# Window attention, forward and backward: one 64x64-mode stretch a step instead of two, weights turned straight from DRAM, and weight-gradient tail over five PSUM banks

## The chip, the cores and the metric

The kernel runs on one core of one Trainium2 chip. The metric is the device time of one execution in microseconds (us), the median over several runs. A run's state is "fast" where it agrees with the other runs of its kernel, and "unknown" for a single run; no run of this study fell in the slow state, and the mean granted TensorE clock of a run lies between 0.98 and 1.00 in all of them (it was lower for short stretches, see run 1). TensorE is called PE below, its weight load PEld, VectorE DVE, ScalarE ACT, GpSimd POOL, and SyncE SP. SP computes nothing here; it issues DMAs. PS in the code is PSUM, the memory that TensorE's products are written to: eight banks of 512 columns. To evict a bank is to copy it out by ACT or DVE.

## The reference, cut to what matters

```python
def _fwd_reference(x, wqkv, wo):                 # x (1,256,256,384), 8x8 windows
    xw = ...                                     # (1024 windows, 64 tokens, 384)
    qkv = xw @ wqkv
    q, k, v = ...
    p = _softmax(jnp.einsum('bqc,bkc->bqk', q, k) * C ** (-0.5), axis=-1)
    o = jnp.einsum('bqk,bkc->bqc', p, v) @ wo
    return ...                                   # back to (1,256,256,384)

def reference(x, wqkv, wo, grad_out):            # all bf16
    _out, _vjp = jax.vjp(_fwd_reference, x, wqkv, wo)
    return (_out, *_vjp(grad_out))               # out, dx, dwqkv, dwo
```

The kernel folds the weights once (A = scale Wq Wk^T, B = Wv Wo, and both transposed). It then works on 128 "quads" of four tiles; a tile is two windows, 128 tokens by 384 channels.

## The kernel before

Each turn of the loop ("step n") works on three quads at once. Quad n (T) gets its outputs, its transposed-attention products and its input gradient, quad n+1 (S) its scores and softmax, and quad n+2 (A) its two projections. SP issues everything that comes in: eight loads of 96 KB a step (four X, four DO), then four DMA transposes, called "turns" here: XT and DOT from the inputs, and two YH turns that turn the projections' results back. POOL issues the stores: four OS stores (out) and eight DXS stores (dx).

```python
def load(n):
    for t in range(4):
        SP.dma_start(out=X[:, (n % NX) * 4 + t, :], in_=img(x, n, t))
        SP.dma_start(out=DO[:, (n % ND) * 4 + t, :], in_=img(grad_out, n, t))

def turn_in(n):            # ... cut: xs, ds are the four tiles of the quad
    SP.dma_start_transpose(out=XT[:, n % NXT, :, :], in_=xs)
    SP.dma_start_transpose(out=DOT[:, n % NDT, :, :], in_=ds)

def turn_yh(n, a):
    SP.dma_start_transpose(out=YH[:, n % NTOK, a, :, :], in_=YHT[...])

def proj(n, a, banks, engs):   # three PSUM banks, each evicted to YHT by its engine
    ...
def attn(n, t, bvw, bdx):      # 64x64 mode: eight 64x384 products of one tile
    ...
def step(n):
    T, S, A = n, n + 1, n + 2
    ...                        # cut: load(n + 4), turn_in(n + 3)
    scores(S); chain1(S); md(T)
    wgrad(g, k0)               # 12 products into bank 7
    chain2(S); chain3(S)
    outs(T, 0, 0, ACT); outs(T, 2, 2, DVE); outs_st(T)
    proj(A, 0, (4, 5, 0), (ACT, DVE, ACT)); turn_yh(A, 0)
    wgrad(g, k0 + 1)
    attn(T, 0, 2, 4); attn(T, 1, 0, 5)          # first 64x64 stretch
    dxs(T, 0, 4, ACT); dxs_st(T, 0)
    proj(A, 1, (2, 3, 1), (DVE, ACT, DVE)); turn_yh(A, 1)
    turn_p(S)                                   # second 64x64 stretch ...
    attn(T, 2, 2, 4); attn(T, 3, 0, 5)
    dxs(T, 2, 4, ACT); dxs_st(T, 2)
```

(The conditions for the first and last steps and the evictions of VW are cut. `scores` and `chain1` to `chain3` make the softmax and its gradient; `md` makes the factor MD, from which `outs` makes the output and `dxs` a part of dx; `attn` makes the rest of dx and VW, from which `wgrad` sums the weight gradients. In 64x64 mode, `64*64` in the trace, TensorE's array works as four parts of 64 rows by 64 columns.)

## Time and profile before

The time is 2079.63 us, median of three runs (2079.23 to 2081.49). These lines of the profile's page give the span, the busy time of each engine with its share, then the busy tenths of the 16 DMA engines in 40 slices, the shares of the engines in the chain of work that ended last, and for the OS stores their number, size and median time in us from issue to landing.

```profile
span 2072.7 us, 65934 instructions
PE 2029.9 (98%) x26970; PEld 1149.4 (55%) x26970; DVE 1358.6 (66%) x2452; ACT 985.1 (48%) x1555; POOL 1012.9 (49%) x1798
DMA  8999999999999999999999999999999999999991
PE 96%; DMA 2%; SPq 2%; DVE 0%; ACT 0%; issue 0%; DVEq 0%
out_dram<-OS POOLq DMA_DIRECT2D x512, 96.0 KB, 2.9
```

PE: 98% busy and 96% of the chain. The waits of PE for the turned input are few, as this line of the waits view says (us in total, times, longest), and all five fall before 100 us:

```profile
PE PS L73 <- DMA XT<-X: 10.2, 5, 3.5
```

The DMA row stands at 9 in nearly every slice. The timeline of SP's queue in one steady step (start, length of the issue):

```profile
1001.81 5.21 SPq L101 DMA_TRANSPOSE YH<-YHT  x2
1007.08 0.59 SPq L91 DMA_DIRECT2D X<-in_x_dram  x1
1007.75 0.55 SPq L92 DMA_DIRECT2D DO<-in_grad_out_dram  x1
...
1011.68 0.55 SPq L92 DMA_DIRECT2D DO<-in_grad_out_dram  x1
1012.28 2.47 SPq L96 DMA_TRANSPOSE XT<-X  x1
1014.80 2.58 SPq L98 DMA_TRANSPOSE DOT<-DO  x1
```

A load takes SP about 0.6 us, a turn 2 to 3 us, and each issue starts within some 0.1 us of the end of the one before. (The time that SP waits for another engine lies before such a record and not in it: in run 4, where SP does wait, the second YH turn is recorded from 0.025 us after the end of the eviction that it needs, in all of 90 steps looked at.)

Here are the stages of one step, the mean over the middle steps, from the start of one stage's first product to the start of the next. They are worked out from the start times of the products in the trace.

| stage | before, us | after, us |
|---|---|---|
| scores | 0.878 | 1.180 |
| md | 0.797 | 0.797 |
| wgrad, first | 1.960 | 1.960 |
| outs | 1.950 | 1.950 |
| wgrad, second | 2.043 | 2.460 (1.950 when nothing waits) |
| proj0 | 1.943 | 2.043 |
| 64x64 stretches | 0.777 and 1.214 | 1.987 |
| dxs | 0.987 and 1.079 | 1.976 |
| proj1 | 2.036 | 2.036 |
| whole step, mean | 15.66 | 16.38 |

The mode switches hide in the last product of a stage: 128x384 products follow each other at 0.162 us, but the last one before a 64x64 stretch takes 0.256.

### The profile page before, as it was taken

What the parts mean: (1) busy time and instruction counts of PE and PEld (TensorE: products, weight loads), DVE (VectorE), ACT (ScalarE), POOL (GpSimd) and SP (SyncE); (2) the same over time, 40 slices, a digit from 0 to 9 for tenths busy, and PEclk for the clock granted to TensorE, in tenths of its full rate; (3) what the DMA queues carried; (4) which work ended last, traced back from release to release, by engine and by line L of the source; (5) the groups of instructions that cost most, each with busy time, mean ns of one, the idle gap of its engine ahead of it and who ended that gap; (6) DMA issues with size and microseconds to landing.
All of it is one profiled execution on the core that took longest, in us unless ns stands there. A gap on an engine that the chain in (4) does not pass through costs nothing.

```text
span 2072.7 us, 65934 instructions
## 1 busy us (share of the span) xinstructions
PE 2029.9 (98%) x26970; PEld 1149.4 (55%) x26970; DVE 1358.6 (66%) x2452; ACT 985.1 (48%) x1555; POOL 1012.9 (49%) x1798
## 2 busy tenths in 40 slices
PE   5899999999999999999999999999999999999997
PEld 2455555555555555555555555555555555555554
DVE  3566666666666666666666666666666666666664
ACT  2444444444445444444444444544444444444452
POOL 1454555555555455455555555545545555555552
PEclk9999999999999999999999999999999999999999
DMA  8999999999999999999999999999999999999991
GB/s 177 203 202 202 208 201 197 209 205 198 205 207 200 204 206 200 202 209 198 206 200 205 203 204 203 202 203 205 200 201 208 202 201 204 206 204 200 206 177 56
DMA packets 1030734, 410.90 MB, mean 198 GB/s; under 512 B 865056, under 2 KB 1013280, under 8 KB 1030432
## 3 DMA queue, kind: packets, MB, share of 16 engines
q1 hardware_dynamic: 956304, 305.37, 84.1%
q0 software_dynamic: 73728, 101.02, 18.2%
q8 instruction: 212, 3.47, 0.7%
q14 instruction: 90, 0.74, 0.1%
q10 hardware_dynamic: 400, 0.29, 0.0%
HBM read 101.84 MB, written 101.84 MB: 98 GB/s over the span
## 4 chain that ended last, share of the span: by engine, by line
PE 96%; DMA 2%; SPq 2%; DVE 0%; ACT 0%; issue 0%; DVEq 0%
PE PS L73 94%; PE PS L150 2%; DMA XT<-X 1%; SPq L92 0%; SPq L91 0%; SPq L231 0%; DMA VW<-in_wo_dram 0%; DVE ACC L219 0%; SPq L233 0%; ACT DXS L77 0%; ACT YHT L77 0%; SPq L98 0%; DVE YHT L79 0%; SPq L96 0%; PE PS L310 0%
## 5 line engine op out<-in xcount | busy, mean ns | idle before, releaser
L207 POOL DMA_DIRECT2D out_dram<-DXS x1024 | 572.8, 566 | 583.7 <-ACT DXS L77 561.4
L73 PE MATMUL PS<-VW,X 128*128 128x384 bf16 x3072 | 542.7, 326 | 4.5 <-DVE ACC L219 4.5
L73 PEld LDWEIGHTS <-X 64*64 64x64 bf16 (+1 forms) x9216 | 380.3, 104 | 218.8 <-issue 6.9
L79 DVE CAST YHT<-PS 128x512 bf16<-128x512 f32 x384 | 264.3, 688 | 240.4 <-PE PS L73 238.4
L73 PEld LDWEIGHTS <-MD 128*128 128x128 bf16 x3072 | 279.3, 98 | 232.4 <-issue 61.5
L77 ACT CAST VW<-PS 128x768 bf16<-128x768 f32 x256 | 204.3, 798 | 367.6 <-PE PS L73 367.6
L77 ACT CAST YHT<-PS 128x512 bf16<-128x512 f32 x384 | 224.7, 585 | 277.6 <-PE PS L73 253.7
L219 DVE TENSOR_TENSOR ACC<-PS,ACC 128x384 f32<-128x384 f32 x252 | 140.5, 558 | 257.3 <-PE PS L73 257.3
L73 PE MATMUL PS<-AT_sb,MD 128*128 128x384 bf16 x1536 | 294.1, 328 | 0.0
L141 POOL TENSOR_TENSOR UM<-PB,ST 128x256 f32<-128x256 bf16 x128 | 77.8, 608 | 424.1 <-PE PS L73 367.8
L73 PE MATMUL PS<-XT,A_sb 128*128 128x512 bf16 x1152 | 273.7, 383 | 10.4 <-DMA XT<-X 10.2
L177 POOL DMA_DIRECT2D out_dram<-OS x512 | 276.1, 545 | 13.9 <-issue 11.4
L73 PE MATMUL PS<-B_sb,MD 128*128 128x384 bf16 x1536 | 271.5, 326 | 4.3 <-DVE MD L79 2.5
L73 PE MATMUL PS<-DOT,BT_sb 128*128 128x512 bf16 x1152 | 270.5, 380 | 0.0
L77 ACT CAST DXS<-PS 128x768 bf16<-128x768 f32 x256 | 204.3, 798 | 138.3 <-PE PS L73 138.3
L79 DVE CAST VW<-PS 128x768 bf16<-128x768 f32 x256 | 244.0, 953 | 18.6 <-PE PS L73 4.8
L79 DVE CAST MD<-PS 128x512 bf16<-128x512 f32 x384 | 240.2, 681 | 0.6 <-PE PS L73 0.6
L73 PE MATMUL PS<-YH,PB 64*64 64x384 bf16 x2048 | 238.6, 332 | 1.0 <-ACT DXS L77 1.0
L77 ACT CAST MD<-PS 128x512 bf16<-128x512 f32 x384 | 200.1, 594 | 67.1 <-DVE ST L128 64.6
L77 ACT CAST OS<-PS 128x768 bf16<-128x768 f32 x128 | 102.1, 798 | 194.5 <-PE PS L73 194.5
L73 PEld LDWEIGHTS <-A_sb 128*128 128x128 bf16 x1152 | 113.4, 99 | 135.6 <-issue 12.4
L73 PEld LDWEIGHTS <-BT_sb 128*128 128x128 bf16 x1152 | 113.1, 98 | 123.8 <-issue 2.4
(46 smaller groups left out, 1618.6 us busy)
## 6 DMA issues: line engine op xcount, KB each, us to landing
X<-in_x_dram SPq DMA_DIRECT2D x512, 96.0 KB, 3.1
DO<-in_grad_out_dram SPq DMA_DIRECT2D x512, 96.0 KB, 3.2
out_dram<-OS POOLq DMA_DIRECT2D x512, 96.0 KB, 2.9
out_dram<-DXS POOLq DMA_DIRECT2D x1024, 48.0 KB, 3.8
YH<-YHT SPq DMA_TRANSPOSE x256, 5.4
XT<-X SPq DMA_TRANSPOSE x128, 6.6
DOT<-DO SPq DMA_TRANSPOSE x128, 6.5
w_sb<-in_wqkv_dram SPq DMA_DIRECT2D x3, 288.0 KB, 4.0
```

The costliest lines, as they stand in the source:

```text
L73: PE.matmul(out, lhsT=lhsT, rhs=rhs, start=start, stop=stop, skip_group_check=True)
L77: ACT.copy(out=out, in_=in_)
L79: DVE.tensor_copy(out=out, in_=in_)
L141: POOL.tensor_tensor(out=UM[:], in0=pb[:, 1], in1=bcast(3), op=ALU.mult)
L150: PE.transpose(bb[r, t * P + a * 64:t * P + a * 64 + 64], PB[r, n % 2, a, t, :], ident[r, r])
L177: POOL.dma_start(out=img(out_0, n, t), in_=OS[:, n % 2, t, :])
L207: POOL.dma_start(out=img(out_1, n, t)[8 * w:8 * w + 8], in_=DXS[64 * (1 - w):64 * (1 - w) + 64, n % 2, t, :])
L219: DVE.tensor_tensor(out=ACC[:, k, :], in0=PS[:, 7, 0:C], in1=ACC[:, k, :], op=ALU.add)
```

## The change

The intent is fourfold. All four tiles' 64x64 products and turn_p go into one stretch, which saves a pair of mode switches. For this the accumulators of dx are packed without regard to bank edges, and products that cross an edge are split (18 more products a step). The first weight products shall start earlier: wqkv is turned straight from DRAM, and the first loads go out on three queues. And the wgrads at the end alternate over five banks instead of waiting for the eviction of one.

```diff
+    PSF = PS[:].rearrange("p b c -> p (b c)")
@@ proj: the third bank of proj0 is evicted in halves
+            if engs[mo] is None:
+                ev(ACT, YHT[:, n % NYH, a, mo, 0:256], o[:, 0:256])
+                ev(DVE, YHT[:, n % NYH, a, mo, 256:512], o[:, 256:512])
@@
+    def mmf(f, rows, lhsT, rhs, start, stop, alone=False):
+        c = 0
+        while c < C:                      # split at bank edges
+            k = min(C - c, 512 - (f + c) % 512)
+            mm(PSF[rows, f + c:f + c + k], lhsT, rhs(c, c + k), start and (alone or (f + c) % 512 == 0), stop)
+            c += k
+    def attn_all(n, S):
+        fvw = ((3072, 3584), (1536, 1920), (2304, 2688), (3072, 3584))
+        for t in range(4):
+            attn(n, t, 0, fvw[t][0], t * C)
+            ...                           # cut: VW of tile 1 to ACT
+            attn(n, t, 1, fvw[t][1], t * C)
+            if t == 0:
+                ev(ACT, VW[:, v, 0, :], PSF[:, 3072:3456])
+                ev(DVE, VW[:, v, 1, :], PSF[:, 3584:3968])
+        ...                               # cut: other evictions, turn_p(S)
@@ step
-            proj(A, 0, (4, 5, 0), (ACT, DVE, ACT)); turn_yh(A, 0)
-            wgrad(g, k0 + 1)
-            attn(T, 0, ...); attn(T, 1, ...); dxs(T, 0, ...)
-            proj(A, 1, (2, 3, 1), (DVE, ACT, DVE)); turn_yh(A, 1)
-            turn_p(S)
-            attn(T, 2, ...); attn(T, 3, ...); dxs(T, 2, ...)
+            wgrad(g, k0 + 1)
+            proj(A, 0, (3, 1, 2), (ACT, DVE, None)); turn_yh(A, 0)
+            attn_all(T, S)
+            dxs(T)
+            proj(A, 1, (3, 4, 5), (ACT, DVE, ACT)); turn_yh(A, 1)
@@ start (cut)
-            SP.dma_start(out=w_sb[:, m, :], in_=wqkv[m * P:(m + 1) * P, :])
+            SP.dma_start_transpose(out=wT[:, :, m * P:(m + 1) * P], in_=wqkv[m * P:(m + 1) * P, :])
+            ACT.dma_start(...)            # quad 0
+            POOL.dma_start(...)           # quad 1
+            if n == 2:                    # in the loop, three times each:
+                    SP.dma_start(out=w_sb[:, m, :], in_=wqkv[m * P:(m + 1) * P, :])
+                    SP.dma_start_transpose(out=woT_sb[:, :, m * P:(m + 1) * P], in_=wo[m * P:(m + 1) * P, :])
@@ end (cut)
+            wgrad(n // GQ - 1, 2 * (n % GQ) + i, (3, 4, 5, 6, 7)[b % 5])
```

(The lines are joined where they were long. Warm-up products at the start, a bf16 accumulator for the last group, and a spread of the final products over ACT and DVE are cut.)

## The prediction

> **What bounds it now.** The page gives PE 98% busy and 96% of the chain that ended last; in steady state PE waits for no DMA. The PE timeline repeats every 15.66 us. One step, start to start: scores 0.88, md 0.80, wgrad 1.96, outs 1.95, proj0 1.94, wgrad 2.04, attn(0,1) 0.78, dxs 0.99, proj1 2.04, turn_p plus attn(2,3) 1.21, dxs 1.08. 128x384 matmuls follow each other at 0.162 us, but at 0.256 into 64x64 mode and 0.255 out of it: a switch costs about 0.09 us. The Trainium skill ("TensorEngine Tiling (Array Packing)", Key Properties) says that changing mode drains the array; the trace agrees. In attn(2,3) the last DO products start 0.315 us after the products before them (0.16 lost), waiting for DVE's eviction of proj1's third bank.
>
> **What changes per step.** Two 64x64 stretches merge: one pair of switches less. Now 2.17 us (0.09 in, 0.78, 0.09 in, 1.21). After: 0.09 in, 8 products per array tile at 0.162 plus 0.02, turn_p on the diagonal tiles 8 x 0.032, 0.10 out: about 1.79. Gain 0.38, of which 0.16 is the vanished wait. Splitting at bank edges adds 18 matmuls with weight loads (12 in 64x64, 6 in dxs); 128-column matmuls run at 0.056 us with loads hidden, so about 3 ns each: 0.03 us. Products of different tiles overtake each other now (YH products start before earlier transposes), so pieces on one tile should not hold up the others.
>
> **What it moves.** proj1 becomes the last work of a step, and scores of the same data follow at once. The first step of the kernel before has this order: last proj1 start 30.52, scores 30.83, 28 products, then a gap 31.265 to 31.681 for the third bank's eviction (DVE 0.69). With ACT (0.585) I expect 0.30 us lost each step. The fourth tile's product into bank 6 also waits for ACT, which first evicts half of proj0's last bank (0.44) and VW (0.51): about 0.1 us. Sum: -0.38 +0.03 +0.30 +0.10 = +0.05 us a step, +6 us over 128 steps, all on PE, so all critical.
>
> **Prologue and tail.** First matmul 13.97 us now; with weights turned straight from DRAM and loads from three queues, about 9. But SP issues some 13 us per step (8 loads of 0.6, two input turns of 1.7, two YH turns of 2.2), and the first steps without wgrad stay bound by it; so I take the shift at the third proj0 start: 48.3 to about 36, gain 12. Tail: 18.4 us of wgrads with 0.65 waits become 11.7, plus about 1 from the ACC copies. Gain 7.5.
>
> **Prediction.** 2079.6 + 6 - 12 - 7.5 = about 2066 us; range 2043 to 2090. Faster by over 2%: 0.13; within 2%: 0.83; slower: 0.04.
>
> **What would show it.** Right: step near 15.7; one 64x64 stretch of 1.8 to 1.9 us; a gap near 0.33 between score products 28 and 29, and waits of PE on ACT YHT; 18 more matmuls a step with no time of their own; first weight products near 9 us; tail wgrads without gaps. Wrong: a stretch of 2.2 us or more (pieces queue in order), dxs well over 1.97 us (splits cost), no gap in scores.
>
> **What would make it wrong.** If scores do not wait, the step is 15.4 and the time 2030, over 2% faster. If split pieces block other tiles, or later YH turns make DMA (busy in nine tenths of every slice) bind, up to 0.5 us a step is lost: 2100 or more.

## The result and the profile after

The changed kernel takes 2152.6 us, median of four runs (2143.34 to 2154.43), beside 2079.43 for the kernel before (2074.55 to 2081.49). The ratio is 1.0346, with a 95% interval of 1.0312 to 1.0381: slower by 3.5%, well outside the predicted range. Ratios here are the mean time of one kernel's fast runs over that of the other's of the same rounds, so they are not quite the ratio of the medians quoted.

The same lines of the page:

```profile
span 2151.1 us, 70961 instructions
PE 2055.3 (96%) x29288; PEld 1267.7 (59%) x29288; DVE 1465.2 (68%) x2705; ACT 940.2 (44%) x1681; POOL 1018.6 (47%) x1806
DMA  9999999999999999999999999999999999999993
PE 74%; DMA 19%; ACT 4%; SPq 2%; issue 1%; DVE 0%; POOL 0%; ACTq 0%
out_dram<-OS POOLq DMA_DIRECT2D x512, 96.0 KB, 4.8
```

The chain is the line to read. PE fell from 96% to 74% of it, and DMA rose from 2% to 19%, nearly all of it the XT turn. The OS stores take 4.8 us to land instead of 2.9. The waits view says how often PE stood, and how often for the eviction that the scores need:

```profile
PEld L74 <- DMA XT<-X: 85.4, 79, 6.7
PE PS L74 <- DMA XT<-X: 55.9, 55, 6.3
PEld L74 <- ACT YHT L78: 28.1, 125, 0.2
```

A long wait appears in the row of the weight load as well as in that of the product, so the first two lines are not to be added. The timeline shows one such place: SP is at its YH turns, the four OS stores are going out, and proj0 waits for an XT that was issued before them.

```profile
1128.23 5.56 SPq L102 DMA_TRANSPOSE YH<-YHT  x2
1129.32 2.16 POOL L183 DMA_DIRECT2D out_dram<-OS  x4
1130.31 1.90 PE L74 MATMUL PS<-XT,A_sb 128*128 128x512 bf16 x8 [1.18 <-DMA XT<-X]
```

**Where the 78 us went.** In the two profiled runs (2072.7 and 2151.1) the first score product starts at 30.83 before and at 26.34 after, the last step's scores at 2017.68 and 2103.70. So the start gains 4.5 us (part of it because 3.1 us of weight products now come after those scores), the end after those scores gains 7.6 (55.0 to 47.4), and the 127 steps between lose 90.5, or 0.71 us each. Wgrad number two is 2.460 long with the wait of proj0 in it and 1.950 without, so the wait for XT costs 0.51 us a step on average, 65 us in all. The wait isn't even: 62 of the 123 steps looked at wait over 0.15 us. And 6.5 of the 65 us are a single stall, which ends at 114.86 us and belongs to the new start (run 1). The rest, 0.21 us a step or 27 us, is PE's own: the scores grew by 0.302, and everything else together shrank by 0.09.

**The scores** show the predicted gap. This is the timeline:

```profile
1022.06 1.25 PE L74 MATMUL PS<-XT,YHT 128*64 128x64 bf16 x48
1022.17 0.59 ACT L78 CAST YHT<-PS 128x512 bf16<-128x512 f32 x1 [0.71 <-PE PS L74]
1022.80 0.39 PEld L74 LDWEIGHTS <-YHT 128*64 128x64 bf16 x20 [0.22 <-ACT YHT L78]
```

The last 20 weight loads start at 1022.80, when ACT's eviction of proj1's last bank (1022.17 + 0.59) is done.

**The stretch** was to be 1.79 us with the switch into it, and is 2.08 (1.987 plus 0.093 that lies in proj0's last product). It was 2.17 in the two parts of before. Its timeline tells why:

```profile
1016.16 0.37 ACT L78 CAST YHT<-PS 128x256 bf16<-128x256 f32 x1 [0.71 <-PE PS L74]
1016.45 0.48 ACT L78 CAST VW<-PS 128x384 bf16<-128x384 f32 x1
1016.57 0.42 DVE L80 CAST YHT<-PS 128x256 bf16<-128x256 f32 x1 [0.30 <-ACT YHT L78]
...
1016.91 0.55 DVE L80 CAST VW<-PS 128x384 bf16<-128x384 f32 x1
1017.05 0.30 PE L74 MATMUL PS<-YH,PB 64*64 64x128 bf16 x2
...
1017.27 0.46 PE L74 MATMUL PS<-YH,PB 64*64 64x384 bf16 x3
1017.51 0.35 PE L74 MATMUL PS<-DO,PB 64*64 64x384 bf16 x2
```

DVE's half of proj0's third bank doesn't run beside ACT's half. It starts at 1016.57, just after ACT's 1016.16 + 0.37 is over, and the line names the ACT eviction as its releaser. The Trainium skill ("PSUM — Partial Sum Buffer", section "PSUM bank collisions raise a hardware error") says that two engines must not access one bank and quadrant (a quarter of the partitions) at the same time, and that the compiler back end's scheduler adds a dependency between them; the trace has such a wait, whoever put it there. It has it at a second place: DVE's eviction of the third VW tile begins in the bank in which ACT's eviction of the second ends, and starts at 1017.94, after 0.48 us of waiting and 0.03 us after the end of ACT's (1017.11 + 0.80). No run reads the halves from two banks, so that the shared bank is the reason is not shown apart from this. The split eviction is over at about 1016.99. ACT alone, by an estimate, would have been done at 1016.16 + 0.585 = 1016.75 (0.585 us is what ACT needs for a whole bank in this trace). The YH product at 1017.05, which writes that bank, waits for it, and DVE's eviction of VW, and with it the fourth tile's DO product at 1017.51, moves back too.

**SP's queue.** This table is worked out from the trace's issue records of the middle steps (mean length of the issue in us, and its median start, counted from the start of the scores that began last):

```
                 before            after
                 length  start     length  start
first X load     0.84    7.8       1.10    12.2
other 7 loads    0.56 to 0.63      0.57 to 0.80
XT turn          2.14    13.4      2.37    2.0
DOT turn         2.67    15.6      2.62    4.5
YH turn, a = 0   2.84    2.6       1.98    7.1
YH turn, a = 1   2.02    5.7       2.85    9.0
```

At the least, a load takes 0.54 and a turn 1.4 to 1.8 (the minima of each row in the trace). The OS stores hardly moved: nine in ten are issued 7.9 to 9.5 us after the scores' start before and 8.2 to 9.8 after, and land some us later. It is SP's cycle that lies 3 to 5 us later, which fits the new order, since proj0 needs XT 2 us later in the step and its YH turn comes later with it. So the same stores fell among SP's loads before and fall on the last YH turn after. That turn grew, but the first YH turn shrank by as much. Summed over a step, SP's turns went from 9.7 to 9.8 us and its loads from 5.0 to 5.6 us. So most of the 0.7 us by which SP's cycle grew lies in the loads behind that turn, and the longer turn alone doesn't explain it.

### The profile page after: what moved, and what is told of

Same layout as the page of the kernel before. It is cut to its first block, busy times and chain, and to the rows that moved or that the text cites. A ratio compares the mean times of both kernels' runs of the same rounds, so it can differ in the third digit from the quotient of the medians.

```text
span 2151.1 us, 70961 instructions
## 1 busy us (share of the span) xinstructions
PE 2055.3 (96%) x29288; PEld 1267.7 (59%) x29288; DVE 1465.2 (68%) x2705; ACT 940.2 (44%) x1681; POOL 1018.6 (47%) x1806
## 4 chain that ended last, share of the span: by engine, by line
PE 74%; DMA 19%; ACT 4%; SPq 2%; issue 1%; DVE 0%; POOL 0%; ACTq 0%
PE PS L74 73%; DMA XT<-X 18%; ACT YHT L78 3%; PE PS L156 1%; SPq L93 1%; SPq L92 1%; DMA DO<-in_grad_out_dram 0%; DMA VW<-in_wqkv_dram 0%; DMA out_dram<-DXS 0%; ACT VW L358 0%; DVE ACC L253 0%; ACT DXS L78 0%; POOL out_dram L241 0%; PE PS L368 0%; SPq L102 0%
## 5 line engine op out<-in xcount | busy, mean ns | idle before, releaser
L78 ACT CAST YHT<-PS 128x512 bf16<-128x512 f32 (+1 forms) x512 | 272.8, 533 | 654.1 <-PE PS L74 653.3
L74 PEld LDWEIGHTS <-MD 128*128 128x128 bf16 x3840 | 332.7, 98 | 151.8 <-ACT MD L78 4.5
L80 DVE CAST YHT<-PS 128x512 bf16<-128x512 f32 (+1 forms) x384 | 231.4, 603 | 220.5 <-PE PS L74 174.5
L80 DVE CAST VW<-PS 128x384 bf16<-128x384 f32 (+1 forms) x384 | 252.1, 684 | 62.8 <-ACT VW L78 61.9
L74 PE MATMUL PS<-AT_sb,MD 128*128 128x384 bf16 (+2 forms) x2304 | 273.8, 273 | 0.0
L78 ACT CAST VW<-PS 128x384 bf16<-128x384 f32 (+1 forms) x384 | 224.8, 586 | 43.3 <-PE PS L74 28.5
L74 PE MATMUL PS<-YH,PB 64*64 64x128 bf16 (+2 forms) x3072 | 229.0, 273 | 0.0
L74 PEld LDWEIGHTS <-A_sb 128*128 128x128 bf16 x1152 | 107.5, 99 | 202.2 <-DMA XT<-X 85.4
L74 PEld LDWEIGHTS <-PB 64*64 64x64 bf16 x5632 | 162.0, 106 | 93.5 <-issue 80.0
L80 DVE CAST DXS<-PS 128x768 bf16<-128x768 f32 x128 | 122.6, 958 | 104.2 <-ACT DXS L78 104.2
```

Of the source, the lines that this page charges most:

```text
L74: PE.matmul(out, lhsT=lhsT, rhs=rhs, start=start, stop=stop, skip_group_check=True)
L78: ACT.copy(out=out, in_=in_)
L80: DVE.tensor_copy(out=out, in_=in_)
```

## The experiments

Fourteen kernels ran. The kernel before, in the same rounds, had medians of 2076.2 to 2077.0. The changed kernel was not run again beside them; as the kernel before differs by 3 us, differences from the changed kernel are good to some us.

### 1. The old loop with the new start and end (b_protail)

The edit takes the changed kernel and puts back the old `turn_p`, `attn`, `dxs` and order of `step`.

> The old step order and old 64x64 products, with the new prologue and the new tail. Both theories: the third proj0 starts 4.7 us earlier in the changed kernel than before, and from the last dxs to the end it takes 23.0 us against 30.9; so about 12 us faster than before (2067 us), step 15.66 us, and no wait of proj0 for XT in the steady steps. If instead the new prologue itself leaves the DMA queue a step late for good, waits for XT appear here too and the time is above 2079.

It took 2071.29 us, ratio 0.9979 (0.9964 to 0.9994): 5 us of the 12 expected. The trace says where the rest is: the first scores start 5.0 us earlier than before (25.80), the end is 8.0 us shorter, but the loop between is 8.75 us longer, although its middle steps are exactly as before (15.66). The timeline has the place:

```profile
96.19 0.58 SPq L326 DMA_DIRECT2D w_sb<-in_wqkv_dram  x1
96.82 1.24 SPq L327 DMA_TRANSPOSE woT_sb<-in_wo_dram  x1
...
100.58 1.25 SPq L327 DMA_TRANSPOSE woT_sb<-in_wo_dram  x1
101.88 0.59 SPq L92 DMA_DIRECT2D X<-in_x_dram  x1
...
107.97 1.68 SPq L97 DMA_TRANSPOSE XT<-X  x1
...
113.61 1.01 PE L74 MATMUL PS<-XT,A_sb 128*128 128x512 bf16 x2 [6.50 <-DMA XT<-X]
```

The six issues that the change moved from the start into step 2 hold SP's queue for 5.7 us (96.19 to 101.88), the XT turn behind them comes late, and PE stands 6.5 us. The stall also costs after it has ended: the trace's granted clock of TensorE is 0.50 from 112.5 to 119.3 us, and the products of this proj0 follow each other at 0.427 us instead of 0.216, some 3 us more by an estimate from these steps and those of the wgrad behind it. The earlier start was given back here: the scores of quad 5 start 5.3 us earlier than before, those of quad 6 4.1 us later. (No run takes the six issues alone away.) The end's gain is the whole gain; the start with the loop behind it lost 3.7 us.

### 2. Without the YH turns (a_noyh, wrong result)

```diff
     def turn_yh(n, a):
+        if not n < 3:
+            return
```

> The changed kernel with the two YH turns left out from quad 3 on (wrong result on purpose): two DMA transposes a step less. Theory D (the in-order SP queue and the DMA engines deliver a turned X only every 16.4 us, later than PE wants it): waits of proj0 for XT vanish, step falls from a mean of 16.38 to the 15.88 that the stages of PE add up to without that wait, total about 2090. Theory P (the loss is PE's own, new waits on evictions): step and total hardly change (2140 or more).

2088.09 us. The step is 15.87, PE's own work, and the waits for XT are gone but for the first steps. So the supply of data is what costs the 0.51 us, and the 12 us that remain over the kernel before are of the size of PE's own +0.21 us a step (27 us) less the gains at the start and the end (12). Which part of the supply (the issue on SP, or the DMA engines behind it) this run can't say, as it relieves both.

### 3. md ahead of the scores (a_mdfirst)

```diff
+        if doT:
+            md(T)
         if doS and S > 0:
             scores(S)
             chain1(S)
-        if doT:
-            md(T)
...
-            proj(A, 1, (3, 4, 5), (ACT, DVE, ACT))
+            proj(A, 1, (3, 4, 7), (ACT, DVE, ACT))
```

> The changed kernel with md ahead of scores in a step and the last bank of proj1 moved from 5 to 7, so scores no longer wait 0.30 us for an eviction. Theory P: 0.30 us a step less, 38 us in all, about 2114. Theory D: the gap between score products 28 and 29 goes, but proj0 waits for XT that much longer; step stays near 16.4 and the total within 10 us of 2152.

It took 2123.15 us, ratio 1.0231 (1.0216 to 1.0246). The gap in the scores is gone (0.881 long, it was 1.180), but the step fell only from 16.38 to about 16.2: the wait of proj0 grew a little (wgrad number two is about 2.5 long). Two thirds (by the step) to three quarters (29 of 38 us of time) of a saving on PE came through, which neither expectation had. PE and the supply are coupled, and not by SP waiting for PE: SP pauses no more than before (0.06 us a step in gaps over 0.15 us). No run takes the coupling apart.

### 4. The DO loads issued by POOL (a_dopool)

```diff
-            SP.dma_start(out=DO[:, (n % ND) * 4 + t, :], in_=img(grad_out, n, t))
+            POOL.dma_start(out=DO[:, (n % ND) * 4 + t, :], in_=img(grad_out, n, t))
```

> The changed kernel with the four DO loads of a step issued by POOL instead of SP: same bytes, 2.5 us less issue on SP a step. Theory D by issue (the SP queue is what is full): waits for XT vanish, step near 15.9, total about 2090. Theory D by bandwidth (the 16 engines are what is full): waits stay, step above 16.2, total above 2130. Theory P: no change.

It took 2085.36 us, ratio 1.0045 (1.0029 to 1.0062): 67 us less than the changed kernel, with one word changed. The chain is PE's again:

```profile
PE 93%; ACT 4%; DMA 2%; DVE 1%; issue 1%; SPq 0%; ACTq 0%; DVEq 0%
```

The step is 15.87. SP, which had no idle time, now has some 3.3 us a step before its second YH turn (in the issue records that turn is issued 5.42 us after the first, which took 2.10). The DMA engines have not become less busy: the packets' time is 97.8% of 16 engines in the changed kernel's 2151.1 us and 101.5% in this one's 2086.4, some 2104 and 2118 us (the two large queues' shares added). So what bound was SP's queue and not the sum of work on the 16 engines: the time that SP takes to issue, or the order in which its one queue is served. This run relieves both, and no run tells them apart. The first reading agrees with the Trainium skill ("Perfetto Trace Analysis", section "DMA Optimizations"), which advises balancing over sync, scalar and GPSIMD where descriptor generation is the bottleneck, and with "Trainium Kernel Development and Optimization" (section "Key Constraints"), by which several issuing engines share the same 16 DMA engines and save only the issue time. Here four loads a step taken off SP were worth 67 us.

### 5. Both (c_best1)

The edits of 3 and 4 together.

> Both repairs together: DO loads issued by POOL, and md ahead of scores with proj1's last bank in 7. If the two losses are separate (SP queue, and the eviction before scores), they add: no wait for XT, score gap gone, step 15.57 us, total about 2047. If POOL's loads or the DMA engines become the next limit, XT waits come back and the total stays above 2070.

It took 2050.59 us, ratio 0.9873 (0.9858 to 0.9888), with a step of 15.57 as expected. With SP relieved, the whole 0.30 us of md first arrives.

### 6. And one engine for one bank (c_best2)

```diff
-                ev(ACT, VW[:, v, 0, :], PSF[:, 3072:3456])
-                ev(DVE, VW[:, v, 1, :], PSF[:, 3584:3968])
+                ev(DVE, VW[:, v, 0, :], PSF[:, 3072:3456])
+                ev(ACT, VW[:, v, 1, :], PSF[:, 3584:3968])
...
-            proj(A, 0, (3, 1, 2), (ACT, DVE, None))
+            proj(A, 0, (3, 1, 2), (ACT, DVE, ACT))
...
-            SP.dma_start_transpose(out=wT[:, :, m * P:(m + 1) * P], in_=wqkv[m * P:(m + 1) * P, :])
+            SP.dma_start(out=w_sb[:, m, :], in_=wqkv[m * P:(m + 1) * P, :])
+        for m in range(CK):
+            SP.dma_start_transpose(out=wT[:, :, m * P:(m + 1) * P], in_=w_sb[:, m, :])
```

(The loads of w_sb in step 2 are dropped with it, and the warm-up products are 22 instead of 14.)

> c_best1, and the last bank of proj0 evicted whole by ACT (the two halves on ACT and DVE were serialized on one bank) with the first product's VW halves swapped between DVE and ACT; and the weights loaded to SBUF first and turned from there. Expected: the 64x64 stretch falls from 1.99 to about 1.80 us, step 15.39; the first weight product starts near 10 us instead of 16.9; total about 2018. If the stretch is limited by the split pieces instead of that eviction, it stays at 1.99.

It took 2017.83 us (2017.48 to 2019.63), ratio 0.9718 (0.9702 to 0.9734), correct. The stretch is 1.70 us after the switch into it, 1.79 with it: exactly the length that the prediction had given the change. In the timeline it runs from the first of these lines to the last, 1000.00 to 1001.70, with turn_p's transposes (the third line here) at its end and no wait in between:

```profile
1000.00 0.35 PE L74 MATMUL PS<-X,PB 64*64 64x384 bf16 x2
...
1001.17 0.35 PE L74 MATMUL PS<-DO,PB 64*64 64x384 bf16 x2
1001.33 0.44 PE L156 MATMUL PS<-ident,PB 64*64 64x64 bf16 x16
1001.70 2.14 PE L74 MATMUL PS<-AT_sb,MD 128*128 128x384 bf16 x18
```

The step is 15.28, 0.375 us below before. That is what the merge is worth when nothing is lost elsewhere. The start missed its expectation by far: the first weight product starts at 24.28 us. The weight turns were issued at 4.09, but had to share the DMA engines with 16 loads on ACT's and POOL's queues:

```profile
4.09 13.18 SPq L319 DMA_TRANSPOSE VW<-w_sb  x3
24.28 4.80 PE L74 MATMUL PS<-VW 128*128 128x384 bf16 x18 [16.85 <-DMA VW<-w_sb]
```

In the kernel before the same three turns took 4.32 us to issue. By this reading, which run 11 tests, the three-queue loads bought issue time and paid for it with the one transfer that everything waits for.

### 7. Without the OS stores (a_noos, wrong result)

```diff
     def outs_st(n):
+        if n >= 3:
+            return
```

> The changed kernel without the OS stores from quad 3 on (wrong result on purpose): the SP queue issues exactly the same, the DMA engines move a quarter less, and nothing of POOL's OS burst meets the turns. Theory contention (turns issue slowly because stores share the engines): waits for XT vanish, total about 2090. Theory issue alone (SP's own instruction time): waits stay, total above 2140.

2098.36 us; the mean step is 15.91 and nearly no XT wait is left. So issue on SP isn't all: with the same issues on SP, fewer bytes from another queue are enough. What SP issues took 14.95 us a step in all, beside 15.44 in the changed kernel: its issues are stretched by what else the DMA engines carry.

### 8. The kernel before with less PE work (b_nowg, wrong result)

```diff
-            if doF:
+            if doF and not 0 < g < NG - 2:
                 wgrad(g, k0 + 1)
```

> The kernel before with every second wgrad of the middle steps left out (wrong result on purpose): PE has 2.04 us less a step, 13.62. If the SP queue of the kernel before had room to spare, the step falls to 13.6 and the total to about 1825. If it was about to bind (XT landed only 0.4 to 2.8 us before its use), the step falls only to 15 or a little more, total 2000 or more, with waits for XT.

2087.5 us, not less than before, with some 2 us of products fewer in each step. By subtraction the step would be 13.62 (run 12 shows that 14.15 is what PE takes when it doesn't wait for XT); it is 15.75. This is the wait, beside 10.2 us in 5 times in the kernel before:

```profile
PE PS L73 <- DMA XT<-X: 162.5, 100, 3.5
```

This is the run that settles the reading of the profile of before. Its loop on SP had a pace of its own of about 15.7 us, the same as PE's 15.66. PE was the limit by a hair. (The mean granted clock was 0.981 here: after longer waits the trace has it at 0.50, for 3.4 us as a rule. That is an estimate of 0.019 x 2085.6 = 40 us of full-speed time, so SP's own pace may lie somewhat below 15.7.)

### 9. OS stores later in the changed kernel (a_oslate)

```diff
             outs(T, 2, 2, DVE)
-            outs_st(T)
...
             dxs(T)
+            outs_st(T)
```

> The changed kernel with the four OS stores issued after the eight DXS stores instead of before them: same stores, same bytes, same SP queue; only their time moves, from the turns (where they are in the changed kernel) to the loads. Theory collision (the store burst that falls into the turns makes them slow): waits for XT shrink, total 2120 or less. Theory total load (only the sum of DMA work counts): total within 15 us of 2152.

It took 2191.65 us, ratio 1.0559 (1.0542 to 1.0577): worse, against my expectation. The burst of stores didn't land among SP's loads, where I had aimed it, but was issued 3.2 to 6.5 us after the next step's scores began, later than aimed, and so on the DOT and first YH turns. These are longer by 0.78 and 0.63 us (3.40 from 2.62, 2.61 from 1.98). The aim was wrong, the sensitivity to the aim is the finding.

### 10. Without the DXS stores (a_nodxs, wrong result)

```diff
     def dxs_st(n, t0):
+        if n >= 3:
+            return
```

> The changed kernel without the DXS stores from quad 3 on (wrong result on purpose): the same number of bytes as a_noos left out (2098 us there), but of stores that fall mostly into the load phase of SP. Theory collision: waits for XT mostly stay, total above 2125. Theory total load: as with a_noos, total about 2098.

2100.16 us, step 15.87, no steady XT waits. Half of the stores taken away is enough, whichever half. This speaks for the sum of the load, and against the idea that the OS stores alone do the harm.

### 11. A start with the weights first (c_best3)

```diff
+        ACT.dma_start(out=wo_sb[:], in_=wo.rearrange("(m p) n -> p m n", p=P))
         for t in range(4):
             ACT.dma_start(out=X[:, t, :], in_=img(x, 0, t))
-        ACT.dma_start(out=wo_sb[:], in_=wo.rearrange("(m p) n -> p m n", p=P))
...
-        for t in range(4):
-            POOL.dma_start(out=X[:, 4 + t, :], in_=img(x, 1, t))
-            POOL.dma_start(out=DO[:, 4 + t, :], in_=img(grad_out, 1, t))
         make_identity(nc, ident[:])
         turn_in(0)
+        for t in range(4):
+            SP.dma_start(out=X[:, 4 + t, :], in_=img(x, 1, t))
+            SP.dma_start(out=DO[:, 4 + t, :], in_=img(grad_out, 1, t))
         turn_in(1)
```

> c_best2 with quad 1's first loads issued on SP behind the weight turns, not on POOL ahead of them; weight load of wo ahead of X on ACT. If the weight turns were late (landed at 24 us) because the other queues' loads share the DMA engines with them, the first weight product starts near 14 us as in the kernel before, and the total is about 2009. If not, it stays at 24 us and 2018.

It took 2015.3 us (2013.04 to 2015.85), ratio 0.9703 (0.9689 to 0.9718), correct, and is the best kernel: 3% faster than before. The first weight product starts at 13.71 instead of 24.28, as expected, but only 2.5 us of the 10.6 arrive (4.7 between the two profiled runs). The third proj0 waits, and its nine products then take 4.02 us instead of 2.10, at a granted clock of 0.50 (42.4 to 49.2):

```profile
13.71 5.42 PE L74 MATMUL PS<-VW 128*128 128x384 bf16 x18 [5.82 <-DMA VW<-w_sb]
43.40 4.02 PE L74 MATMUL PS<-XT,A_sb 128*128 128x512 bf16 x9 [5.39 <-DMA XT<-X]
```

Once more an earlier start of PE is given back at the next place where it needs SP.

### 12. Less PE work and DO on POOL (b_nowg_dopool, wrong result)

The edits of 8 and 4 on the kernel before.

> b_nowg (which did not get faster: mean step 15.75 us, waits for XT) with the DO loads of a step on POOL. If SP's own issue was the limit of the kernel before as well, the step falls to between 13.6 and 14.5 us and the total to 1830 to 1950. If the DMA engines' bandwidth was, it stays above 15.3 and 2030.

1881.95 us, a step of 14.15, and this wait:

```profile
PE PS L73 <- DMA XT<-X: 1.8, 2, 1.0
```

The same work on PE as in 8, and 205 us less. So it was SP's queue that limited the kernel before as soon as PE got faster.

### 13. OS stores later in the kernel before (b_oslate)

By now two readings were left of what makes the changed kernel's loop slower than 15.7: the place of the store bursts in SP's cycle, or something else in the new order. This run moves the stores and nothing else, in the kernel before.

```diff
                 outs(T, 2, 2, DVE)
-                outs_st(T)
...
                 dxs_st(T, 2)
+                outs_st(T)
```

> The kernel before with the four OS stores issued after the step's DXS stores: PE order, SP queue and bytes unchanged; the OS burst moves from SP's load phase (7.8 to 13.4 us after the start of scores, where the trace shows it at 8.5 to 12) to about 3 to 6 us, into the DOT and YH turns. Theory collision: those turns take longer, XT comes late, waits for XT appear on PE and the total rises above 2095. If the time of a store burst does not matter, total 2076.

It took 2186.25 us, ratio 1.0521 (1.0497 to 1.0546). The same bytes, issues and products, with four stores a step issued some 11 us later (3.4 to 5.9 us after the next scores' start, on SP's DOT and first YH turns), cost 110 us. The chain and the wait look like those of the changed kernel:

```profile
PE 74%; DMA 21%; SPq 4%; issue 1%; DVE 0%; ACT 0%; DVEq 0%
PE PS L73 <- DMA XT<-X: 95.4, 70, 4.6
```

The issue of the DOT turn grew from 2.67 to 3.0 us, of the first YH turn from 2.84 to 3.1, and of the second from 2.02 to 2.4. All turns of a step took 10.6 us instead of 9.7, and the loads 5.0 as before: here the lengthened turns are the whole loss.

### 14. OS stores in SP's load phase, in the changed kernel (a_osmid)

The stores are held back until the last VW tile is written, by a copy of one column on POOL. That puts their issue at 12.7 to 15.0 us after the scores' start, where SP issues loads (10.5 to 15.8 in this run).

```diff
             attn_all(T, S if doS else None)
+            POOL.tensor_copy(out=SCR[:], in_=VW[:, (T % NVW) * 4 + 3, 0, 0:1])
+            outs_st(T)
             dxs(T)
```

> The changed kernel with the OS stores held back on POOL (behind a one-column copy that reads the last evicted VW tile) so that they are issued about 12.5 to 15 us after the start of scores, in SP's load phase, and no longer at 9 to 12, in the second YH turn. Theory collision: the second YH turn falls from 2.85 toward 2.0 us, waits for XT shrink, total 2125 or less. If the time of the burst does not matter, total within 10 us of 2152.

It took 2117.14 us, ratio 1.0198 (1.0181 to 1.0215), 35 us less than the changed kernel with the same work. The second YH turn takes 1.79 us to issue instead of 2.85, and the OS stores land in 2.9 us instead of 4.8, as they did before:

```profile
out_dram<-OS POOLq DMA_DIRECT2D x512, 96.0 KB, 2.9
PE PS L75 <- DMA XT<-X: 23.7, 34, 2.7
```

So about half of the 65 us of XT wait is the place of this burst. The shorter second YH turn isn't how it was won, though: the other three turns grew by as much (the turns of a step sum to 9.8 us in both), and what shrank are the loads, from 5.6 to 5.3 us a step.

## Why the prediction was wrong

**The step that failed** is "in steady state PE waits for no DMA", read as "all on PE, so all critical". The observation was right, the conclusion wasn't: no wait isn't the same as room to spare. XT landed only 0.4 to 2.7 us before its use in nine of ten steady steps of the kernel before (landing records of the trace), SP's queue had no idle time, and taking 2 us of PE's work away gained nothing (run 8). The loop on SP stood at the same pace as PE's. With the new order the OS stores no longer meet SP's loads but its last turn, SP's cycle grew longer than PE's own 15.87 us, and PE waits 0.51 us a step, 65 us with the stall after the start. Runs 2, 4, 7 and 10 each take the wait away by relieving the supply, run 14 takes half of it by moving the stores (with one small copy on POOL), and run 13 makes such a wait in the kernel before by moving them. The prediction itself had named this among what would make it wrong ("later YH turns make DMA ... bind, up to 0.5 us a step is lost"), with the right size; it gave it too little chance. It had even counted "some 13 us" of issues of SP a step for the start, with turns at 1.7 and 2.2 us. The trace has 2.0 to 2.8, and the sum fills the step.

**The stretch** was mis-sized: 2.08 us against 1.89 (1.79 and the 0.1 foreseen for the fourth tile's wait). That term should have been about 0.3, since the two half-evictions of one bank follow each other. The difference of 0.19 us a step makes 24 us. Run 6 agrees: with the whole bank on ACT, and the first tile's two VW evictions swapped between DVE and ACT, the stretch is 1.79. It makes both edits at once, so it doesn't say what each is worth.

**The start** was mis-sized, and in its worth wrong: first weight products at 16.93 us, not near 9, and third proj0 at 43.54, not 36. Worse, what is gained there is lost by step 6, by the timeline of run 1 to the six issues put into SP's queue. Of the 12 us expected none is left there.

**What held.** The mode switch of 0.09 us: the merged stretch of run 6 saves 0.375 us a step in all, against 0.38 predicted. The Trainium skill's "TensorEngine Tiling (Array Packing)", section "Key Properties", says that a change of mode drains the array; it has no number, the trace gives 0.256 against 0.162. The gap in the scores: 0.30 predicted, 0.302 measured. The splits: dxs takes 1.976 us against 1.95 for twelve unsplit products (outs), so they cost next to nothing. The end: 7.5 predicted, 7.6 to 8.0 measured, without gaps in the 72 wgrads:

```profile
2128.09 11.86 PE L74 MATMUL PS<-VW,X 128*128 128x384 bf16 x72
```

**What stays open.** That the place of the stores matters is shown, and so is that their amount matters (runs 7 and 10). Why the changed loop settles at 16.38 us and not at, say, 16.0 isn't settled: a late XT moves PE's phase against SP's, and with it the next stores, and no run takes this feedback apart. By which of SP's issues the store burst delays XT is open too, as the loads grew more than the turns. Nor does any run tell how much of a turn's length on SP is its own work and how much is waiting for the DMA engines to take it.

## What to carry to other kernels

Before you call an engine the only limit, look at the slack of what feeds it: how long before its first use a transfer lands, and whether the queue that issues it is ever idle; a queue without idle time may be a second limit, which a run with less work on the engine will tell, and the cheapest remedy here was to issue part of its transfers from another engine. When an order changes, ask where the bursts of stores fall in the cycle of that queue: here moving four stores a step from the loads to the transposes cost 5%. Give one PSUM bank's eviction to one engine, note that pauses of TensorE of 5 to 7 us cost more than their length here (runs 1 and 11), and don't let early transfers crowd the one that the first product waits for.

## What the Trainium skill lacked or had wrong

- "DMA: Bandwidth & Descriptors" has no time, measured on this chip and beside other transfers, for what an issue costs the issuing engine. Here a plain 96 KB load takes SP 0.55 to 0.6 us, and a transpose of a quad 1.4 to 1.8 us at the least and, with other transfers running, 1.6 to 3.4 us on average.
- No page has that stores from another queue lengthen the issue of transposes: with four stores a step issued some 11 us later, on SP's turns, the turns of a step took 10.6 us instead of 9.7, and the kernel 5.2% longer (run 13).
- "Trainium Kernel Development and Optimization", section "Key Constraints", says that issuing from several engines only saves issue time. No run here shows more than that, but it was worth 67 us of 2152 (run 4), and there is a price at the start that it doesn't name: the weight turns delayed the first product to 24.28 us beside 16 loads on other queues, and to 13.71 with fewer (runs 6 and 11).
- "TensorEngine Tiling (Array Packing)", section "PSUM Bottleneck", advises to use both ScalarE and VectorE for evacuation. It should add "not on one bank", as the PSUM page has it: the two halves ran one after the other (0.37 and then 0.42 us), and the whole bank on ScalarE takes 0.585. Its "Key Properties" have no figure for a mode switch; the runs show 0.09 us.
